# Seven block products for eight in the down projection of a gated feed-forward, and the feed-forward cut into an up phase and a down phase for each half of the tokens

## The chip, the core and the metric

The kernel runs on one core of one Trainium2 chip. The metric is the device time of one execution in microseconds (us); the median of the runs counts. TensorE (PE in the profile) does the matrix products, ScalarE (ACT) the activation functions and plain copies, VectorE (DVE) and GpSimd (POOL) the elementwise work, and SyncE (SP) issues nearly all DMAs, one after the other, from one queue. PE writes its sums into PSUM, which has 8 banks of 128 x 512 fp32 numbers; everything else lies in SBUF or in DRAM.

## The reference, cut to what matters

```python
xn = _layernorm(x)                    # x: 2048 tokens x 640
s  = _A_ref(xn, wqkv, w_phi, wo)      # 32 heads of linear attention: softmax features of q and k, then @ wo
h  = gelu(xn @ w1 + b1)               # 640 -> 1536
g  = silu(h @ w2 + b2)                # 1536 -> 640
return x + s * g
```

All of it is fp32. The kernel computes each large product to nearly that precision with three passes of the faster fp32r format: an operand a is kept as `hi` (a rounded to fp32r) and `lo = a - hi`, and the product is hi*hi + hi*lo + lo*hi. So every operand of a large product needs a copy (`hi`, on ACT) and a subtraction (`lo`, on DVE or POOL) before PE can use it, and PE runs three matmuls for one product of 128 x 128 weights with 512 columns.

## The kernel before, in words

Time runs in three stages.

The **first stage** normalizes and transposes x and computes k, v and q and the features of k and q. It ends with the exponentials of q in DRAM (`e_dram`) and with x in two forms in SBUF: `xp` (the eight blocks of x, as hi and lo) and `xd` (nine sums and differences of those blocks). One half of the tokens (1024) lies there at a time; both halves are also in DRAM (`xp_dram`, `xd_dram`).

The **feed-forward stage** is a loop over 12 units: 2 halves of the tokens times 6 groups `g` of 256 of the 1536 hidden features. The order of all instructions on all engines is the order in which the program writes them; nothing is reordered. A unit has two parts.

- Up: the 256 x 640 by 640 x 1024 product for the group, as seven block products for eight (Strassen's scheme in Winograd's form) over two column blocks of 512 tokens and two of 128 features. `PARTS` lists the seven; `part` (L1191 to L1202) issues 6 matmuls for a block product, 9 where the odd fifth block of 128 of the 640 is added: 54 in a unit. ACT and DVE put the results together (`keep` L1217, sums at L1488 to L1508), `act` (L1205) applies the Gelu in the PSUM bank and copies the `hi` part to SBUF, and `act_lo` (L1212) subtracts, with PSUM as one source.
- Down: `down` (L1222 to L1240) multiplies the group's 256 hidden features with w2, for 512 tokens and then for the other 512, into five blocks of 128 outputs: 2 x 5 x 2 x 3 = 60 matmuls. Each of the ten results of a unit is only a partial sum over 256 of 1536 features, so DVE adds it to a running sum `y` in SBUF (L1239; a plain copy, L1237, in the first group).

Beside that run, spread over the unit with generators that `next` advances: the w2 weights of a unit are loaded whole and split by ACT and POOL (L136, L138); the w1 weights of the next unit are loaded and their sums and differences formed and split (L589 to L601; in the second half most come back from DRAM instead, `w1_back`); the queries of 16 token tiles are normalized (`q_norm`, L1285: two products over 128 x 1280 on POOL, two sums over heads and some small work on DVE) and stored as `phi_dram`; at the end of the first half `reload` brings the second half of x from DRAM; after it the gates of the first half go through the Silu to `g_dram` (L1472).

The **last stage** goes over four chunks of 512 tokens. `num_t` (L1324, L1327) transposes the query features, `num_m` (L1335 to L1339) multiplies them with the state of the keys, `finish` (L1402 to L1405) multiplies with wo (15 matmuls for one of five output blocks), by the gate, and adds x. The first chunk's transposes and state products lie inside the last unit's down part (`last_mid`), as do the splits of wo.

SBUF is given out from pools of equal buffers: `slabs` (23 of 5 KB per partition), `rows` (11 of 2.75 KB), and `xp`, `xd`. A tile that finds no free buffer waits until an older tile's last reader is done, and what is queued behind it on its engine, or on SP, waits too.

## Time and profile before

| | |
|---|---|
| time, median of 3 runs (lowest, highest) | 661.1 us (660.86, 661.21) |
| profiled execution, from the first to the last instruction | 659.8 us |
| PE busy, PE weight loads busy | 652.2 us, 572.6 us |
| DVE, POOL, ACT busy | 449.2, 392.8, 325.4 us |
| DMA, mean over the span | 198 GB/s |
| feed-forward stage, from the chain of waits | 238.42 to about 559.7 us |

The profiled execution's own time is given only as its span; the runs' median stands 1.3 us above that span. A row of the groups of instructions reads: line, engine, operation, output tile <- input tiles, shape, count | busy time, mean duration of one | idle time of that engine just before them and who ended it. Matmuls overlap, so the mean duration of one (about 390 ns) is not the time that one adds; the chain of waits, which merges successive work of one line into a piece with a start, a length and a count, gives that.

### The profile page before, as it was taken

Reading aid. Unit: us, or ns where it says so; the run is one execution under the profiler, and the core shown is the slowest. Engines: PE = TensorE matmul, PEld = TensorE weight load, DVE = VectorE, ACT = ScalarE, POOL = GpSimd, SP = SyncE. Lnnn points to the kernel's source line nnn. Section 1 sums busy time; section 2 is a strip of 40 time slices with the busy share of each in tenths; the row PEclk is TensorE's granted clock in tenths of the full one; section 3 lists DMA queues with packets and bytes.
Section 4 is the critical chain, followed back from the end, with each engine's and each line's share of the span. In section 5 each row is a group of like instructions: output and inputs, shape, how many; then the busy total and the mean of one; then the engine's idle time right before and its main releaser. Section 6 shows DMA issues by size and latency. Waiting matters only on the chain.

```text
span 659.8 us, 11974 instructions
## 1 busy us (share of the span) xinstructions
PE 652.2 (99%) x4616; PEld 572.6 (87%) x4616; DVE 449.2 (68%) x714; ACT 325.4 (49%) x550; POOL 392.8 (60%) x344
## 2 busy tenths in 40 slices
PE   8999999999999999999999999999999999999997
PEld 8999999999999998888888888888888887877876
DVE  5878987766885756595885685777967877333132
ACT  4556777644666678435245138632132336645320
POOL 3597887774883437776875754746357665422322
PEclk9999999999999999999999999999999999999999
DMA  8436912031924882539656697456375275668444
GB/s 319 184 121 205 294 63 67 27 102 37 299 87 147 312 310 81 198 118 321 222 178 246 249 425 290 167 223 243 120 283 199 81 307 230 209 215 316 139 133 148
DMA packets 77081, 130.62 MB, mean 198 GB/s; under 512 B 5056, under 2 KB 44480, under 8 KB 76128
## 3 DMA queue, kind: packets, MB, share of 16 engines
q1 hardware_dynamic: 76704, 129.20, 55.0%
q10 hardware_dynamic: 320, 0.66, 0.6%
q8 instruction: 36, 0.59, 0.3%
q14 instruction: 21, 0.17, 0.1%
HBM read 81.66 MB, written 46.20 MB: 194 GB/s over the span
## 4 chain that ended last, share of the span: by engine, by line
PE 94%; POOL 2%; DMA 1%; issue 1%; DVE 1%; ACT 0%; SPq 0%; POOLq 0%
PE pB L1230 25%; PE pB L1201 22%; PE pW L485 20%; PE pB L1402 10%; PE pA L344 4%; PE pW L977 3%; PE pB L1335 3%; PE pB L1324 2%; PE pA L163 2%; PE kv L577 1%; DMA folds<-in_wqk_dram 1%; POOL tt L276 1%; POOL xd L295 0%; PE pB L1342 0%; PE pA L330 0%
## 5 line engine op out<-in xcount | busy, mean ns | idle before, releaser
L1230 PE MATMUL pB<-hs,w2s 128*128 128x512 f32 x720 | 167.0, 390 | 0.0
L1230 PEld LDWEIGHTS pB<-hs,w2s 128*128 128x128 f32 x720 | 134.6, 188 | 28.2 <-DVE oT L1339 0.4
L1201 PE MATMUL pB<-xp,w1s 128*128 128x512 f32 x324 | 81.3, 389 | 0.0
L1201 PE MATMUL pB<-xd,w1s 128*128 128x512 f32 x324 | 79.3, 389 | 0.0
L1239 DVE TENSOR_TENSOR y<-pB,y 128x512 f32<-128x512 f32 x100 | 63.7, 680 | 15.8 <-PE pB L1230 15.6
L1402 PE MATMUL pB<-oT,wo 128*128 128x512 f32 (+1 forms) x315 | 72.5, 385 | 0.2
L1201 PEld LDWEIGHTS pB<-xd,w1s 128*128 128x128 f32 x324 | 60.8, 188 | 12.6
L1201 PEld LDWEIGHTS pB<-xp,w1s 128*128 128x128 f32 x324 | 60.8, 188 | 12.6
L1206 ACT ACTIVATE pB<-pB,b1t 128x512 f32<-128x512 f32 x48 | 31.8, 662 | 77.6 <-DVE pB L1497 28.3
L1402 PEld LDWEIGHTS pB<-oT,wo 128*128 128x128 f32 x315 | 56.1, 188 | 13.0 <-DVE oT L1339 1.2
L402 POOL TENSOR_TENSOR eq<-eq,rc 128x1280 f32<-128x1280 f32 x16 | 37.9, 2369 | 48.7 <-DVE rc L1301 43.8
L383 POOL TENSOR_TENSOR e<-e,mxs 128x1280 f32<-128x1280 f32 x13 | 30.7, 2372 | 41.4 <-DVE mxs L378 25.7
L389 ACT ACTIVATE e<-e 128x1280 f32<-128x1280 f32 x32 | 40.8, 1274 | 17.9 <-POOL e L383 8.3
L601 POOL TENSOR_TENSOR w1s<-raw,w1s 128x640 fp32r<-128x640 f32 (+1 forms) x18 | 24.9, 1386 | 41.2 <-ACT w1s L600 41.1
L485 PE MATMUL pW<-wsum,xd 128*128 128x320 f32 x288 | 48.4, 310 | 0.0
L1288 POOL TENSOR_TENSOR ez<-eq,zrep 128x1280 f32<-128x1280 f32 x16 | 47.3, 2954 | 0.0
L1217 ACT ACTIVATE x<-pB 128x512 f32<-128x512 f32 x12 | 7.2, 600 | 78.9 <-PE pB L1201 78.9
L485 PEld LDWEIGHTS pW<-wsum,xd 128*128 128x128 f32 x288 | 43.6, 188 | 0.0
L138 POOL TENSOR_TENSOR w2s<-raw,w2s 128x640 fp32r<-128x640 f32 x24 | 37.1, 1567 | 7.1 <-ACT w2s L136 7.1
L402 POOL TENSOR_TENSOR e<-e,rc 128x1280 f32<-128x1280 f32 x15 | 36.1, 2410 | 5.8 <-DVE rc L838 4.2
L1327 ACT ACTIVATE ph<-pB 120x512 f32<-120x512 f32 (+1 forms) x44 | 22.9, 604 | 26.5 <-PE pB L1324 23.8
L1212 DVE TENSOR_TENSOR hs<-pB,hs 128x512 fp32r<-128x512 f32 x48 | 32.0, 685 | 5.2 <-ACT hs L1208 5.0
(216 smaller groups left out, 1282.1 us busy)
## 6 DMA issues: line engine op xcount, KB each, us to landing
raw<-in_w_dram SPq DMA_DIRECT2D x42, 320.0 KB
e_dram<-e SPq DMA_DIRECT2D x16, 640.0 KB
eq<-e_dram SPq DMA_DIRECT2D x16, 640.0 KB
phi_dram<-eq SPq DMA_DIRECT2D x16, 640.0 KB
phi<-phi_dram SPq DMA_DIRECT2D x16, 640.0 KB
xt<-in_x_dram SPq DMA_DIRECT2D x16, 320.0 KB
xres<-in_xt_dram SPq DMA_DIRECT2D x20, 256.0 KB
out_dram<-xres SPq DMA_DIRECT2D x18, 256.0 KB
```

Source lines behind the costliest of these rows:

```text
L138: eng.tensor_tensor(sl[:, 1, :], raw, sl[:, 0, :].bitcast(F32), op=OP.subtract)
L383: eng.tensor_tensor(e3, e3, mx[:, :, None].to_broadcast([P, 64, DH]), op=OP.subtract)
L389: nc.scalar.activation(ef, ef, AF.Exp)
L402: eng.tensor_tensor(e3, e3, rc[:, :, None].to_broadcast([P, 64, DH]), op=OP.mult)
L485: nc.tensor.matmul(self.bank[ch][:, :HALF], self.x(blk, a), w(b), start=new and i == 0, stop=i == len(mms) - 1, skip_group_check=True)
L1201: nc.tensor.matmul(bank[ch][:], tl[:, a, off + wo_:off + wo_ + P], mov(blk, b), start=new and n == 0, stop=n == len(mms) - 1, skip_group_c ...
L1206: nc.scalar.activation(ps, ps, AF.Gelu_apprx_tanh, bias=b1t[:, f:f + 1])
L1212: nc.vector.tensor_tensor(hs[:, 1], ps, hs[:, 0].bitcast(F32), op=OP.subtract)
L1230: nc.tensor.matmul(ps[:], ws[i][:, b, d * P:(d + 1) * P], hs[o][i][:, a, :], start=i == n == 0, stop=(i, n) == (GF - 1, 2), skip_group_che ...
L1239: nc.vector.tensor_tensor(y, ps[:], y, op=OP.add)
L1288: nc.gpsimd.tensor_tensor(zv, ef, zf, op=OP.mult)
L1402: nc.tensor.matmul(ps[:, cols], w, o[:, a, cols], start=n == 0, stop=n == 14)
```

## The change

The down product leaves the loop over groups. For each half of the tokens, `up` runs for all six groups and keeps the Gelu's results in SBUF, unsplit (`raws`); then `down` runs once, over all 1536 features, also in seven block products: the features are cut into the first and the second 128 of each group, four of the five output blocks into two pairs, the 1024 tokens into two blocks of 512. Each block product is 6 groups x 2 output blocks x 3 passes = 36 matmuls, accumulated over all groups in the same two PSUM banks. The fifth output block is done in the plain way, mixed in (72 matmuls in a half, as before). A half then has 7 x 36 + 72 = 324 down matmuls, where it had 360.

What this adds: differences of the kept activations (`T1` to `T4`, on POOL, 24 in a half); for each of 42 operands in a half (7 kinds x 6 groups) a `form`: a copy into a PSUM bank and a `hi` copy on ACT, then `lo` on DVE with the bank as source (the first six of a half go without the bank); sums and differences of w2, formed once, split and stored to DRAM (`s_dram`), from where they are loaded in each half; and the plain parts of w2, loaded and split in each half, with `lo` on DVE. The running sums `y` in SBUF are gone: the ten gates of a half are made in one go from PSUM (`gate_out`) and stored, so all the gates come back from DRAM in the last stage.

The side work is no longer advanced by generators but hung on numbered slots: `when(s, f, ...)` files a call, `tick` runs those of a slot in the order in which they were filed. There are 7 slots in an `up`, one after each block product, and 42 in a `down`, one after each operand. The w1 sums of the first half are now needed every 54 matmuls. In the second half of the feed-forward two of the four w1 tiles of a group are loaded and split again and two come from DRAM. The reload of x is spread over the first `down`, and for 256 of its tokens the nine sums are made again from `xp` on POOL instead of going to DRAM (`plan_x`). Eight of the query tiles are normalized beside the second `up` phase, two beside the first `down`, four beside the second, two in the last stage. The first chunk's transposes stand in slots 27 to 37 of the second `down`, its state products in slot 38, the splits of wo in slots 26 to 38.

The pools change: `slabs` has 10 buffers, 13 more (`lead`) serve only the first stage, and a string `HOMES` says for each allocation of that stage which of the two it takes. `lead` and `rows` are then closed and their room goes to 21 `cells` of 4 KB (activations, operands, w1 tiles) and 6 `halves` of 2 KB.

The diff, cut to its core:

```diff
-    slabs = ctx.enter_context(tc.tile_pool(name="slabs", bufs=23))
-    rows = ctx.enter_context(tc.tile_pool(name="rows", bufs=11))
+    slabs = ctx.enter_context(tc.tile_pool(name="slabs", bufs=10))
+    early = ExitStack()
+    lead = early.enter_context(tc.tile_pool(name="lead", bufs=13))
+    rows = early.enter_context(tc.tile_pool(name="rows", bufs=11))
...
+        pool = slabs if next(homes, "S") == "S" else lead
...
-            nc.scalar.activation(sl[:, 0, :n], src, AF.Copy)
-            nc.gpsimd.tensor_tensor(sl[:, 1, :n], src, sl[:, 0, :n].bitcast(F32), op=OP.subtract)
+            (split or split_now)(src, sl[:, 0, :n], sl[:, 1, :n], nc.gpsimd if lo[len(out)] == "pool" else nc.vector)
...
-    PARTS = (("X", "A11", 0, None), ("Y", "S2", 10, None), ("X", "A12", 2, ("A1k", 4)), ("V", "S3", 12, ("A2k", 7)),
-             ("Z", "S1", 8, None), ("W", "A22", 14, ("A2k", 16)), ("Z", "S4", 5, ("A1k", 7)))
+    PARTS = (("X", "A11", 0, None), ("Y", "S2", 10, None), ("V", "S3", 12, ("A2k", 7)), ("Z", "S1", 8, None),
+             ("X", "A12", 2, ("A1k", 4)), ("W", "A22", 14, ("A2k", 16)), ("Z", "S4", 5, ("A1k", 7)))
...
+    def split_late(src, hi, lo, eng):
+        nc.scalar.activation(hi, src, AF.Copy)
+        after(1, lambda: eng.tensor_tensor(lo, src, hi.bitcast(F32), op=OP.subtract))
...
+    UP0, DN0, UP1, DN1, OUT = 0, 42, 84, 126, 168
...
+    def form(n, lo):
+        k, g = FORMS[n]
+        while k in SUM and (k, g) not in sums_done:
+            sum_step()
+        src = block(k, g)
+        hs = cell((P, 2, CW), F32R, "hs")
+        if lo == "bank":
+            ps = bankB()
+            nc.scalar.activation(ps[:], src, AF.Copy)
+        nc.scalar.activation(hs[:, 0], src, AF.Copy)
+        ring[k, g] = hs
+        def low():
+            (nc.gpsimd if lo == "pool" else nc.vector).tensor_tensor(
+                hs[:, 1], ps[:] if lo == "bank" else src, hs[:, 0].bitcast(F32), op=OP.subtract)
+            sums_due.extend([(t, g) for t in dict(B11=("T2",), B21=("T4",), T2=("T1",)).get(k, ())])
+        after(1, low)
...
+    def plan_w(s):
+        for i, k in enumerate(("A11", "A12", "S2", "S3", "S1", "S4", "A22")):
+            for d in range(3):
+                use = s + 6 * i + 2 * d
+                if i == 0:
+                    when(use - 8, w_load, "A5", d)
+                    when(use - 5, w_make, "A5", d)
+                if k in SUMS:
+                    when(use - 6, w_sum, k, d)
+                else:
+                    when(use - 7, w_load, k, d)
+                    when(use - 4, w_make, k, d)
...
+        def step():
+            n = at_step[0]
+            at_step[0] += 1
+            form(n + AHEAD, los(n + AHEAD))        # AHEAD = 6
+            sum_step()
+            tick()
...
+        def run(banks, k, f, start, e=None, lead=0):
+            for g in range(NG):
+                if e is not None:
+                    bank, c, es, et = e
+                    for i in range(lead + 1) if g == 0 else (g + lead,):
+                        if i < NG:
+                            mm3(bank, col("A5", i, c), ring[f, i], es and i == 0, et and i == NG - 1)
+                h = ring.pop((f, g))
+                for i in range(2):
+                    mm3(banks[i], col(k, g, i), h, start and g == 0, g == NG - 1)
+                if g < NG - 1:
+                    step()
...
+    def plan_q(t, s, pace=(-4, 0, 1, 3, 4, 7)):
+        for f, k in zip((q_load, q_ez, q_rc, q_dn, q_scale, q_store), pace):
+            when(s + k, f, t)
...
+    for g in range(1, NG):
+        s = UP0 + 7 * (g - 1)
+        if g > 1:
+            when(s - 4, w1_next, g)
+        when(s + 1, w1_sums, g)
+        for i, k in enumerate((2, 3, 4, 6)):
+            when(s + k, w1_step, g)
+        for i in range(2):
+            when(s + 7 + i, w1_put, g, i)
+    for g in range(NG):
+        plan_s(g, (7, 13, 20, 27, 34, DN0 + 2)[g])
...
+    plan_q(0, DN0 + 5)
+    plan_q(1, DN0 + 9)
...
+    for i in range(4):
+        when(DN0 + 2 + 4 * i, reload, i)
+        when(DN0 + 18 + 4 * i, reload, 4 + i)
```

More of the change, by code (lines that the diff above doesn't have):

```diff
@@ new lines, in add, with when, after, tick @@
+    def add(out, a, b, eng=nc.vector, op=OP.add):
+        eng.tensor_tensor(out, a, b, op=op)
+    todo, at_slot = {}, [0]
+    def when(s, f, *args):
+        assert s >= at_slot[0]
+        todo.setdefault(s, []).append((f, args))
+    def after(k, f, *args):
+        when(at_slot[0] + k, f, *args)
+    def tick():
+        for f, args in todo.pop(at_slot[0], ()):
+            f(*args)
+        at_slot[0] += 1
+    def load(dst, src):
+        nc.sync.dma_start(dst, src)
+    def store(k, dst, src):
+        after(k, load, dst, src)
@@ L1577, in hedgehog_gated_mlp_kernel, with w1_next, w1_step @@
-    hs = (None, (h12, h22))
-    load_res(0)
-    load_res(1)
-    for _ in down(g, w2g, hs, 1, groups):
-        pass
-    for _ in q2:
-        pass
-    gate(0)
-    gate(1)
-    late_store[0] = True
-    for ci, c in enumerate(ORDER):
+            store(1, out_t[d * P:(d + 1) * P, c * CW:(c + 1) * CW], xr[:])
+    def w1_next(g):
+        w1r_at[g] = load_w1(g, lambda *a: slab(a[1], a[2], a[0]))
+    def w1_step(g):
+        out = next(w1f_at[g])
+        if out is not None:
+            w1g_at[g], w1_tiles[g] = out, out["tiles"]
@@ new lines, in hedgehog_gated_mlp_kernel @@
+    for g in range(NG):
+        s = UP1 + 7 * (g - 1)
+        when(s - 3, w1_raw, g)
+        when(s - 1, w1_sum_tiles, g)
+        when(s + 1, w1_wa, g)
+        when(s + 3, w1_wb, g)
+    when(UP1 + 9, kv_state, kvr_out[0])
+    for i in range(8):
+        plan_q(2 + i, UP1 - 1 + 5 * i)
+    down(2, LO)
+    for g in range(NG):
+        up(g)
+    xstack.close()
+    tailp.append(ctx.enter_context(tc.tile_pool(name="late", bufs=8, side="right", reuse_waits="tile")))
+    tailp.append(ctx.enter_context(tc.tile_pool(name="phs", bufs=14, side="right", reuse_waits="tile")))
```

643 lines of the change are left out of this document (342 added, 301 removed).

## The prediction

> **What bounds the kernel now.** First the page: who is busy, and at what clock.
>
> ```profile
> PE 652.2 (99%) x4616; PEld 572.6 (87%) x4616; DVE 449.2 (68%) x714; ACT 325.4 (49%) x550; POOL 392.8 (60%) x344
> PEclk9999999999999999999999999999999999999999
> ```
>
> PE is busy for all but 7.6 us. A busy PE can still be a waiting one, so next the chain of waits in order of time (start, length, piece):
>
> ```profile
> 64.32 2.19 issue
> ...
> 266.47 12.24 PE pB L1201 x54
> 278.71 13.60 PE pB L1230 x60
> ...
> 548.67 0.61 PE pB L1324 x8
> ...
> 556.98 1.62 PE pB L1230 x6
> ...
> 559.02 1.96 DMA oT<-oTl
> 560.99 0.74 ACT wo L136
> ...
> 561.79 1.58 POOL wo L138
> ...
> 563.41 0.73 PE pB L1402 x2
> ...
> 565.35 3.52 PE pB L1402 x15
> ```
>
> In the feed-forward PE alternates between 54 up matmuls and 60 down matmuls without a gap: 12.24 / 54 and 13.60 / 60 both give 0.2267 us for one. That is the price of a matmul of 512 columns in this kernel, whichever operands it has. The busy time by stage says the same:
>
> ```profile
> 252.80:395.70 142.90, 142.90 (x632) 118.20 (x631) 105.35 (x148) 59.14 (x96) 104.67 (x82) 1.00 0.65 235
> 421.90:537.50 115.60, 115.60 (x512) 95.72 (x511) 88.98 (x141) 35.96 (x56) 71.80 (x39) 1.00 0.52 193
> ```
>
> (Columns: stretch, length, PE, PE's weight loads, DVE, ACT, POOL, clock, DMA share, GB/s.) PE 142.90 of 142.90. So a matmul taken out of this stage is worth its whole 0.2267 us, as long as its side work keeps up; DVE and POOL stand at 74% and 73% there, ACT at 41%.
>
> The chain ends the stage with a detour through a DMA, ACT and POOL from 558.60 to 563.41, 4.8 us. It isn't 4.8 us of idle PE, as PE's timeline shows:
>
> ```profile
> 556.91 3.06 PE L1230 MATMUL pB<-hs,w2s 128*128 128x512 f32 x12
> 559.81 4.34 PE L1402 MATMUL pB<-oT,wo 128*128 128x512 f32 x15
> ```
>
> Most of the 15 ran during the detour. Undisturbed, 15 take 3.52 (the chain at 565.35); these end at 559.81 + 4.34 = 564.15 where 556.98 + 12 x 0.2267 + 3.52 = 563.22 was possible. The wait for oT and the last wo costs 0.9 us.
>
> **The change part by part.** *Matmuls.* The down product falls from 12 x 60 = 720 to 2 x (7 x 36 + 72) = 648; up, transposes, state and wo products keep their number. 72 x 0.2267 = **-16.3 us**, all on the path that sets the end.
>
> *End of the feed-forward.* State products and the last wo split move to slot 38 of the second down, with three operands (18 matmuls, 4.1 us) still to run. The 1.96 of the DMA and 0.74 + 1.58 of the split, side by side, fit. **-0.9** (bounds -0.9 to 0).
>
> *Side work* costs nothing where it fits under PE and stalls where it doesn't. Its prices:
>
> ```profile
> L1208 ACT ACTIVATE hs<-pB 128x512 fp32r<-128x512 f32 x48 | 28.8, 600 | 2.1
> L600 ACT ACTIVATE w1s<-st 128x512 fp32r<-128x512 f32 x18 | 10.6, 622 | 0.5 <-POOL st L589 0.5
> L1391 ACT ACTIVATE y<-y,b2t 128x512 f32<-128x512 f32 x10 | 7.0, 724 | 3.0 <-DMA oT<-oTl 3.0
> L1327 ACT ACTIVATE ph<-pB 120x512 f32<-120x512 f32 x40 | 20.9, 606 | 14.0 <-PE pB L1324 11.3 <-issue 2.7
> L136 ACT ACTIVATE w2s<-raw 128x640 fp32r<-128x640 f32 x24 | 16.8, 735 | 11.6 <-DVE dn L397 9.2 <-PE pB L1230 1.7 <-DMA xd_dram<-xhi 0.7
> L1212 DVE TENSOR_TENSOR hs<-pB,hs 128x512 fp32r<-128x512 f32 x48 | 32.0, 685 | 5.2 <-ACT hs L1208 5.0 <-issue 0.2
> L601 POOL TENSOR_TENSOR w1s<-st,w1s 128x512 fp32r<-128x512 f32 x18 | 23.0, 1296 | 0.0
> L589 POOL TENSOR_TENSOR st<-raw 128x256 f32<-128x256 f32 x18 | 13.3, 741 | 7.4 <-DMA w_dram<-w1s 5.0 <-DMA raw<-in_w_dram 2.4
> L1288 POOL TENSOR_TENSOR ez<-eq,zrep 128x1280 f32<-128x1280 f32 x16 | 47.3, 2954 | 0.0
> L402 POOL TENSOR_TENSOR eq<-eq,rc 128x1280 f32<-128x1280 f32 x16 | 37.9, 2369 | 48.7 <-DVE rc L1301 43.8 <-issue 4.9
> ```
>
> *First up phase.* A unit is now 12.24 us, no longer 25.84, and must hold the w1 forms of the next one. POOL: four w1 sums (3.0), two lows (2.6), the w2 sums (four of 256 columns and one of 128, about 3.3), one difference (1.3): 10.2 of 12.24. DVE: five sums of 0.685 (3.4) and lows over 640 + 384 + 2 x 512 + 128 = 2176 columns. These lows have both sources in SBUF, and here two engines get in each other's way:
>
> ```profile
> 168.27 0.83 DVE L138 TENSOR_TENSOR wq<-rq,wq 128x640 fp32r<-128x640 f32 x1
> 169.52 3.82 DVE L138 TENSOR_TENSOR wq<-rq,wq 128x640 fp32r<-128x640 f32 x2 [0.43 <-ACT wq L136]
> 168.94 3.72 POOL L138 TENSOR_TENSOR wq<-rq,wq 128x640 fp32r<-128x640 f32 x2 [2.03 <-ACT wq L136]
> ```
>
> Alone, DVE's subtraction takes 0.83 for 640 columns (1.3 ns each); with POOL at the same work two take 3.82. Undisturbed, 2176 columns are 2.8 us. If they only pass through POOL's gaps, the pair needs 10.2 + 2.8 = 13.0 in 12.24, 0.8 too much, in five units 4.0. The w1 tiles come two to four slots ahead (2.7 to 8 us), which absorbs part. Bounds **0 to 4.0**; I take 1.2, nearer nothing, since a first unit without w2 sums lets POOL get ahead. (The Trainium skill, page "SBUF — State Buffer", section "Who interferes with whom", says that a VectorE tensor_tensor with both inputs in SBUF and a GpSimd operation that reads SBUF exclude each other for a whole instruction. The 3.82 agrees. By the rule the sum would carry the 4.0 in place of 1.2.)
>
> *First down phase* (324 x 0.2267 = 73.4 us of PE, 1.36 or 2.04 a slot). ACT: 36 forms of 0.600 + 0.622 = 44.0, twelve weight copies 7.5, ten gates 7.2, some 3 besides: 62 of 73.4. No row has an ACT copy from SBUF to PSUM; between 0.600 and 0.724, I take 0.600 as the nearest (a plain copy). DVE: 36 x 0.685, twelve lows of 0.67 and a dozen sums are 41, which leaves 32 for the head sums of two query tiles. POOL is the tight one: in the first 18 slots (32.6 us) 18 differences of 1.3 (23.4), a 19th, the last w2 sums (3.3), two query tiles (2 x (2.954 + 2.369) = 10.6): 38.6, so 6 us late at slot 18. The T1 differences filed at slots 12 to 17 are operands at 24 to 29, 20 us later; SP's `q_store` in slot 16 waits for POOL and holds weight loads needed 12.2 us later. DMA moves in these slots, from the shapes, 4.2 MB of x, 3.1 of w2 sums, 2.6 of queries and some 2.8 others: 12.7 MB, 390 GB/s. What it can carry is the reload of before, from 375 to 400 us:
>
> ```profile
> DMA packets 1626, 10.55 MB, mean 422 GB/s; under 512 B 177, under 2 KB 177, under 8 KB 729
> ```
>
> So it is hidden, narrowly: the lead of 12.2 us covers it and POOL's 6, and without that lead each us late would cost one. **0 to 2**, I take 0.3.
>
> *Second up phase*: POOL has one query tile in 9.6 us (5.3) and little else; nothing. *Second down phase*: as the first, plus on ACT the first chunk's copies. In slots 24 to 35 ACT has 12 forms (14.7), two gates (1.4), nine `ph` (5.5), four wo copies (2.9), two weight copies (1.2): 25.7. PE has 20.4 and nine transposes of 0.31 (half of the 0.61 for eight above): 23.2. ACT falls 2.5 behind (3.7 with 0.724 for the copy to PSUM). Operands are made six slots ahead, but a transpose takes a PSUM bank that a late form must give back, so PE can wait here. **0 to 3.7**, I take 1.2.
>
> *First stage.* 23 slabs become 10 and 13 by a fixed list, which can only add waits for a free buffer; two loads to the first unit's w2 go. The nearest price is a transfer of 640 KB, 1.6 us at 422 GB/s. **-1.4 to 3.1** (two such transfers; below nothing, should waits like the 2.19 at 64.32 fall otherwise), I take 0.
>
> *Last stage.* Ten more gate loads (2.6 MB over 91 us), two query tiles, ten Silus fewer on ACT:
>
> ```profile
> 564.20:655.60 91.40, 91.40 (x564) 73.23 (x561) 28.94 (x79) 34.27 (x78) 28.07 (x37) 1.00 0.62 206
> ```
>
> DMA 206 + 29 GB/s, POOL 28 + 11 of 91: nothing.
>
> **Sum**: 659.8 - 16.3 - 0.9 + 1.2 + 0.3 + 1.2 + 0 = 645.3 us for the profiled execution; the median stands 1.3 above the span, so **646.6 us**. The bounds are 643.9 - 1.4 = 642.5 and 643.9 + 4.0 + 2 + 3.7 + 3.1 = 656.7.
>
> **The rivals.** *Nothing stalls*: 661.1 - 17.2 = **643.9**. For it: PE ran gapless with DMA at 422 GB/s and POOL at 73%. Against it: every unit has half the time for w1.
>
> *The first up phase paces itself*: POOL and DVE exclude each other, 13.0 a unit, and the two downs come in at two thirds of their bounds: 643.9 + 4.0 + 3.8 = **651.7**. For it the 3.82 above; against it, that w1 tiles come slots ahead and the first unit gains some 4 us.
>
> *Slower: POOL's queue holds SP.* In the downs everything on POOL is late, `q_store` waits at the head of SP's queue, the reload of `xd` waits for that store, and the weights of S1 and S4 stand behind both. A weight load filed at slot 18 (32.6 us into the phase) is needed 12.2 later and takes some 2, so SP must be free by 42.6. `q_scale`, filed at slot 13 (25.8), takes 2.4: PE stands once POOL is 14 us late there, and then one us for one. I forecast 6. POOL at 1.2 times its rows is 38.6 x 1.2 - 32.6 = 13.7 late, just the point; at 1.43 times 22.6, which costs 8.6 in each down and eats the 17.2. At 1.5 times it is 25.3, 2 x 11.3 = 22.6, **666.5**. For it:
>
> ```profile
> L138 POOL TENSOR_TENSOR w2s<-raw,w2s 128x640 fp32r<-128x640 f32 x24 | 37.1, 1567 | 7.1 <-ACT w2s L136 7.1
> L138 POOL TENSOR_TENSOR wq<-rq,wq 128x640 fp32r<-128x640 f32 x2 | 3.7, 1880 | 2.0 <-ACT wq L136 2.0
> ```
>
> the same operation stretched from 1567 to 1880 beside a DVE at the same work, 1.2 times. Against it: that is the most any row shows.
>
> *The change doesn't do what it says*: side matmuls or stalls spread evenly give the 17 us back, **661**. Counting in the code speaks against it.
>
> **How the numbers follow.** Forecast (645 to 650) 0.48; nothing stalls 0.20; first up phase 0.17; POOL's queue 0.12; no gain 0.03. A difference under 0.2% (1.3 us) can't be told from none. So faster 0.85, same 0.03, slower 0.12. The range takes in the bounds, 642.5 to 656.7, and reaches a little on, to 659; what lies above is most of the last two cases.
>
> **What would show it.** Down matmuls 648 in number and still 0.2267 apart; the down phases as unbroken pieces of 73.4 us, the up phases of 73.4 as well (6 x 12.24). First up phase right: PE's gaps there under 2 us in sum, ended by a w1 tile. Second down: PE waiting before the transposes for ACT, 1 us or so. Wrong: a down phase over 76 us, PE ended by a w2 weight or an operand; SP standing on a store for more than 10 us; matmuls further apart than 0.2267.

## The result, and the profile after

The changed kernel takes 671.4 us (median; 670.28 to 672.46) against 661.15 beside it on the same chip: 1.015 times as long, 95% interval 1.0134 to 1.0165. It is slower; 646.6 was forecast. The page of its profile (busy times; what DMA moved; the chain of waits by engine):

```profile
PE 646.4 (97%) x4544; PEld 559.1 (84%) x4544; DVE 467.2 (70%) x702; ACT 380.3 (57%) x681; POOL 440.2 (66%) x382
...
DMA packets 86411, 154.63 MB, mean 231 GB/s; under 512 B 6320, under 2 KB 47792, under 8 KB 85840
...
PE 70%; DVE 14%; POOL 7%; issue 5%; DMA 2%; ACT 2%; SPq 0%; POOLq 0%; DVEq 0%; ACTq 0%
```

PE has the 72 matmuls less that the change promised (4616 to 4544), yet its busy time fell by 5.8 us only, and 30% of the chain that ended last is no longer PE (6% before). DMA moves 154.63 MB in place of 130.62. Busy time by stage (stretch, length, PE, PEld, DVE, ACT, POOL, clock, DMA share, GB/s), first before: feed-forward, last stage.

```profile
238.20:559.80 321.60, 321.60 (x1469) 264.90 (x1468) 235.64 (x359) 140.24 (x221) 205.77 (x138) 1.00 0.60 222
559.80:655.60 95.80, 95.59 (x580) 75.94 (x578) 32.99 (x84) 37.46 (x81) 29.63 (x38) 1.00 0.60 197
```

After: first up, first down, second up, second down, last stage.

```profile
238.60:314.20 75.60, 75.60 (x326) 60.82 (x326) 52.11 (x66) 49.40 (x81) 66.98 (x64) 1.00 0.78 285
314.20:397.90 83.70, 78.50 (x333) 63.16 (x332) 58.68 (x77) 58.54 (x111) 62.58 (x49) 0.98 0.90 322
397.90:473.90 76.00, 76.00 (x329) 61.11 (x327) 65.14 (x97) 28.42 (x47) 59.10 (x29) 1.00 0.67 247
473.90:564.60 90.70, 84.30 (x414) 66.42 (x413) 72.23 (x102) 65.28 (x125) 56.83 (x33) 1.00 0.79 273
564.60:665.10 100.50, 97.39 (x580) 75.98 (x578) 38.45 (x94) 30.89 (x72) 37.66 (x41) 1.00 0.69 237
```

What PE would need without a stall: 324 x 0.2267 = 73.45 in every phase, in the first down 2.15 more for the eight matmuls of `kv_norm`, in the second up 0.3 for the state's transposes, in the second down 8 for transposes and state products (eleven groups of four transposes at 0.27; 0.56 and 4.32 in the chain). For the last stage, before's 95.8 less its 0.9 of waiting.

| us | first up | first down | second up | second down | last stage |
|---|---|---|---|---|---|
| without a stall | 73.45 | 75.6 | 73.7 | 81.4 | 94.9 |
| forecast | 74.65 | 75.9 | 73.7 | 82.6 | 94.9 |
| after | 75.6 | 83.7 | 76.0 | 90.7 | 100.6 |
| over the forecast | 1.0 | 7.8 | 2.3 | 8.1 | 5.7 |

Together 24.9, where 671.4 - 646.6 = 24.8. (Smaller ones cancel: the median stands 2.4 above the span and not 1.3; the feed-forward of before had itself lost 1.1 against its count of matmuls.) So the question is not where one big loss is, but what five phases lose, each in its way.

**The up phases** have no gap, and yet take longer. PE's timeline (start, length, then what ran) before:

```profile
276.51 2.20 PE L1201 MATMUL pB<-xp,w1s 128*128 128x512 f32 x9
278.55 1.75 PE L1230 MATMUL pB<-hs,w2s 128*128 128x512 f32 x7
```

and after:

```profile
270.09 2.26 PE L1198 MATMUL pB<-xp,w1s 128*128 128x512 f32 x9
272.19 2.26 PE L1198 MATMUL pB<-xd,w1s 128*128 128x512 f32 x9
274.29 3.66 PE L1198 MATMUL pB<-xp,w1s 128*128 128x512 f32 x15
```

From start to start nine matmuls took 2.04 (0.2267 each); now 2.10 (0.2333), at a granted clock of 1.00. The instructions are the same; what differs is where `xp` and `xd` lie. In before, 32 fp32 of padding stood ahead of `xp` (L56, `xpad`), and `xp` and `xd` began at multiples of 256 bytes in each partition. The change drops the padding with the new pools, and both begin 96 bytes beyond one; so do the `wo` weights of the last stage. (These starts follow from the order in which the program gives out SBUF; no profile shows them. The runs below show what shifting them does.)

**The first down** stands three times. The chain of waits there (start, length, piece):

```profile
318.58 10.25 PE pB L1390 x45
...
330.14 1.20 DVE ws L1243
331.34 3.36 DVE w2s L1243
334.70 1.41 DVE rc L404
...
345.79 2.97 POOL qroom L1524
...
348.79 1.50 DVE dn L404
...
351.38 1.17 DVE den L1536
...
353.71 0.69 DVE hs L1313
...
354.44 43.63 PE pB L1390 x184
```

An operand's low part (`hs`, 0.69) stands in DVE's queue behind a query tile's head sum (`dn`), which waits for POOL's product (`qroom`, 2.97). DVE is busy nearly throughout, in the second down too (the first and the last line; the one between is the rest of the first down):

```profile
334.70:355.10 20.40, 15.20 (x64) 11.26 (x63) 18.91 (x27) 13.84 (x25) 16.35 (x11) 1.00 0.76 243
355.10:398.00 42.90, 42.90 (x184) 35.32 (x183) 23.62 (x36) 27.85 (x51) 26.85 (x25) 0.96 0.92 332
...
495.00:515.00 20.00, 16.29 (x71) 12.78 (x70) 19.69 (x25) 11.61 (x21) 19.52 (x13) 1.00 0.72 212
```

DVE 18.91 of 20.40 and 19.69 of 20.00.

PE's waits in the first down come to 5.2 us of the 8.1 lost. Another 1.9 is no wait: the last 184 matmuls fill 43.63 us where 184 x 0.2267 are 41.7. The granted clock is below 1.00 there, as the line between shows (0.96). In steps of 2 us it is 0.50 from 356 to 358, soon after the wait of 2.9 us, 0.69 in the next step, and 1.00 from 360 on. So the low clock comes on top of the wait. The remaining 1.0 us was not placed.

The operation that was costed at 0.67 us, the low part of w2, is among them (group, busy time, mean ns):

```profile
L1243 DVE TENSOR_TENSOR w2s<-w2r,w2s 128x512 fp32r<-128x512 f32 x24 | 27.5, 1150 | 0.6 <-ACT w2s L1242 0.6
```

**The last stage**: PE waits for the transfer of oT, in brackets the wait.

```profile
587.23 3.78 PE L1635 MATMUL pB<-oT,wo 128*128 128x512 f32 x15
592.26 1.94 PE L1635 MATMUL pB<-oT,wo 128*128 128x512 f32 x6 [1.26 <-DMA oT<-oTl]
594.64 2.35 PE L1635 MATMUL pB<-oT,wo 128*128 128x512 f32 x9 [0.44 <-DMA oT<-oTl]
```

The 15 matmuls from 587.23 are done at 591.01; the next wait until 592.26, then until 594.64. One output block, 3.5 us, is all the cover that the transfer has. A third wait for oT, at 621, makes 3.1 us of waiting in all.

### The profile page after: what moved, and what is told of

It reads as the page before. It is cut to its first block, busy times and chain, and to the rows that moved or that the text cites. A ratio compares the mean times of both kernels' runs of the same rounds, so it can differ in the third digit from the quotient of the medians.

```text
span 669.0 us, 12217 instructions
## 1 busy us (share of the span) xinstructions
PE 646.4 (97%) x4544; PEld 559.1 (84%) x4544; DVE 467.2 (70%) x702; ACT 380.3 (57%) x681; POOL 440.2 (66%) x382
## 2 busy tenths in 40 slices
DMA packets 86411, 154.63 MB, mean 231 GB/s; under 512 B 6320, under 2 KB 47792, under 8 KB 85840
## 4 chain that ended last, share of the span: by engine, by line
PE 70%; DVE 14%; POOL 7%; issue 5%; DMA 2%; ACT 2%; SPq 0%; POOLq 0%; DVEq 0%; ACTq 0%
PE pW L492 20%; PE pB L1198 14%; PE pB L1390 13%; PE pB L1635 9%; PE pA L351 4%; POOL ez L1524 3%; DVE dn L404 3%; PE pW L975 3%; DVE w2s L1243 2%; PE pB L1562 2%; PE pA L170 2%; DVE hs L1313 1%; DMA oT<-oTl 1%; PE pB L1573 1%; PE kv L584 1%
## 5 line engine op out<-in xcount | busy, mean ns | idle before, releaser
L1390 PE MATMUL pB<-hs,w2s 128*128 128x512 f32 x648 | 155.1, 396 | 10.6 <-DVE w2s L1243 5.6
L1390 PEld LDWEIGHTS pB<-hs,w2s 128*128 128x128 f32 x648 | 121.0, 189 | 39.6 <-DVE w2s L1243 7.4
L1250 ACT ACTIVATE hr<-pB,b1t 128x512 f32<-128x512 f32 x48 | 32.8, 686 | 68.2 <-DVE pB L1219 67.6
L1638 POOL TENSOR_TENSOR xres<-gt,xres 128x256 f32<-128x256 f32 x36 | 25.7, 735 | 57.2 <-issue 30.6
L1313 DVE TENSOR_TENSOR hs<-pB,hs 128x512 fp32r<-128x512 f32 x72 | 46.6, 678 | 14.1 <-ACT hs L1309 14.0
L1637 DVE TENSOR_TENSOR gt<-pB,gt 128x256 f32<-128x256 f32 x40 | 15.3, 420 | 58.9 <-PE pB L1635 56.0
L1308 ACT ACTIVATE pB<-hr 128x512 f32<-128x512 f32 x72 | 42.2, 586 | 21.9 <-DVE hs L1313 16.6
L1309 ACT ACTIVATE hs<-hr 128x512 fp32r<-128x512 f32 x84 | 52.0, 620 | 4.4 <-PE pB L1390 4.4
L1295 POOL TENSOR_TENSOR hr<-hr 128x512 f32<-128x512 f32 x36 | 50.2, 1422 | 0.0
L1524 POOL TENSOR_TENSOR ez<-eq,zrep 128x1280 f32<-128x1280 f32 x14 | 42.1, 3006 | 1.5 <-PE pB L1390 1.5
```

The lines of the kernel that those rows point to most:

```text
L1250: nc.scalar.activation(dst, ps, AF.Gelu_apprx_tanh, bias=b1t[:, f:f + 1])
L1295: nc.gpsimd.tensor_tensor(block(k, g), block(a, g), block(b, g), op=OP.subtract)
L1308: nc.scalar.activation(ps[:], src, AF.Copy)
L1309: nc.scalar.activation(hs[:, 0], src, AF.Copy)
L1313: (nc.gpsimd if lo == "pool" else nc.vector).tensor_tensor(hs[:, 1], ps[:] if lo == "bank" else src, hs[:, 0].bitcast(F32), op=OP.subtract)
L1390: nc.tensor.matmul(ps[:], w(b), hs[:, a, :], start=start and n == 0, stop=stop and n == 2, skip_group_check=True)
```

## The experiments

Stage lengths are read from PE's timelines as above, the time is the median beside the runs of the kernel before on the same chip (661.2 to 662.2). "Aligned" is the kernel of after with its operands at multiples of 256 bytes again; it is the base of all rows below it.

| us | first up | first down | second up | second down | last | time | ratio, 95% interval |
|---|---|---|---|---|---|---|---|
| after | 75.6 | 83.7 | 76.0 | 90.7 | 100.6 | 671.4 | 1.015 (1.0134 to 1.0165) |
| aligned | 73.7 | 83.1 | 75.5 | 90.9 | 100.8 | 668.6 | 1.010 (1.0073 to 1.0126) |
| aligned, six query tiles not normalized in the downs | 73.7 | 81.7 | 75.5 | 85.2 | 99.0 | 658.8 | 0.9948 (0.9927 to 0.997) |
| the same, and no reload of xp | 73.9 | 75.6 | 75.5 | 85.2 | 98.8 | 655.3 | 0.9906 (0.9887 to 0.9926) |
| aligned, w2's low parts from a bank | 74.9 | 82.9 | 76.4 | 87.5 | 98.1 | 666.0 | 1.0061 (1.0044 to 1.0077) |
| aligned, two blocks of cover | 74.6 | 83.1 | 75.5 | 90.9 | 96.0 | 664.7 | 1.0039 (1.0021 to 1.0056) |
| all three edits, queries 0/9/4/3, lows on POOL | 73.7 | 75.6 | 80.3 | 95.0 | 101.8 | 671.6 | 1.0144 (1.0129 to 1.016) |
| reload later, queries 2/8/4/2 | 74.0 | 81.7 | 77.4 | 85.9 | 95.8 | 659.7 | 0.9962 (0.9947 to 0.9977) |
| queries 0/9/5/2 | 73.6 | 75.7 | 76.3 | 91.4 | 94.9 | 657.1 | 0.9931 (0.9914 to 0.9947) |
| queries 0/9/4/3 | 73.8 | 75.6 | 76.3 | 87.1 | 97.4 | 655.4 | 0.9918 (0.9898 to 0.9938) |
| queries 0/10/4/2 | 74.0 | 78.4 | 75.5 | 89.6 | 95.5 | 658.1 | 0.9948 (0.9931 to 0.9965) |

(Queries a/b/c/d: tiles planned for the first down, second up, second down, last stage.) Stages with the same code differ between these profiles. The first up phases of the aligned kernels lie between 73.6 and 74.9. The last stage with one block of cover and two query tiles goes from 98.1 to 100.8 in five kernels, with two blocks from 94.9 to 96.0 in four. So about a microsecond in an up phase, or less than 3 us in a last stage with one block of cover, is not argued from.

### Where the operands start

The kernel of after with 96 bytes of padding ahead of `xpool`, which puts `xp`, `xd` and `wo` at multiples of 256:

```diff
+    ctx.enter_context(tc.tile_pool(name="pad", bufs=1, side="right")).tile([P, 24], F32, name="rpad")
     xpool = xstack.enter_context(tc.tile_pool(name="xpool", bufs=1, side="right", reuse_waits="tile"))
```

> The changed kernel with 96 bytes of unused SBUF put on the right side ahead of the pool that holds xp and xd, so that xp, xd and later the split wo start at a multiple of 256 bytes as in the kernel before; in the changed kernel they start 96 bytes beyond one. Address theory: the matmuls that stream xp and xd take 0.2333 us there against 0.2267 before because of that start, so each up phase falls from 75.6 to 73.4 us and the finishing products of the last stage from 0.2387 to 0.2347: 2 x 2.2 + 300 x 0.004 = 5.6 us, time 671.4 - 5.6 = 665.8. Rival, load: the matmuls are slowed by the busier DMAs and engines beside them: up phases stay at 75.6 and the time at 671. Both expect the stalls of the down phases to stay.

The kernel of before with more padding, `xp` 96 and `xd` 64 bytes beyond a multiple of 256:

```diff
-    xpool.tile([P, 32], F32, name="xpad")
+    xpool.tile([P, 56], F32, name="xpad")
     xp = xpool.tile([P, 8, 2, CW], F32R, name="xp")
+    xpool.tile([P, 56], F32, name="dpad")
```

> The kernel before with the unused 128 bytes ahead of xp made 224 and 224 more between xp and xd, so that xp starts 96 and xd 64 bytes beyond a multiple of 256; nothing else moves. Address theory: up matmuls at 0.2333 us, a unit's 54 at 12.60 in place of 12.24, 12 units: +4.3 us, 665.4; if only one of the two starts matters, only the matmuls of that tile slow down and the time is 663.3. Rival, load: no change, 661.1.

And once more before, with 64 and 40 in place of 56 and 56 (`xp` 128 bytes beyond, `xd` 32):

> The kernel before with the activations at other starts: xp 128 bytes beyond a multiple of 256 (96 in the run of the first call), xd 32 (64 there). The run with 96 and 64 gave 2.10 us for nine up matmuls on xp (0.2333 each) and 1.39 for six, 3.44 for fifteen on xd (0.2317 and 0.2293), against 0.2267 in the kernel before. If any start off a multiple of 256 costs the same, xp and xd both stay at 0.2317 to 0.2333 and the time is 665 to 667. If the distance from a multiple of 64 or 128 decides, xp at 128 goes back to 0.2267 and xd at 32 stands at 0.229 to 0.233; the time is then 662.5 to 664. All other stages as before.

Aligned, the first up phase of after falls from 75.6 to 73.7 and the time by 2.9 us, where 5.6 was expected; the second falls only from 76.0 to 75.5, since something else holds it there, and the last stage not at all. Before with 96 and 64 takes 666.1 us (ratio 1.0068, 1.005 to 1.0085), a unit 12.53 and not 12.24. With 128 and 32, 665.9 us (1.0065, 1.0048 to 1.0082), a unit 12.57:

```profile
296.00 2.26 PE L1202 MATMUL pB<-xp,w1s 128*128 128x512 f32 x9
298.10 1.56 PE L1202 MATMUL pB<-xd,w1s 128*128 128x512 f32 x6
299.49 0.86 PE L1202 MATMUL pB<-xp,w1s 128*128 128x512 f32 x3
300.19 3.66 PE L1202 MATMUL pB<-xd,w1s 128*128 128x512 f32 x15
303.69 2.26 PE L1202 MATMUL pB<-xp,w1s 128*128 128x512 f32 x9
```

From start to start, nine on `xp` at 128 take 2.10, as at 96, and fifteen on `xd` at 32 take 3.50: 0.2333 both. (At 64 the fifteen took 3.44, 0.2293, and six took 1.39, 0.2317.) Padding and nothing else makes the kernel before 4.4 us slower: the start address is shown as the cause, 32, 96 and 128 cost some 6 to 7 ns a matmul, and "the distance from a multiple of 64 or 128 decides" is out, since 128 costs as much as 96. Why 64 costs less stays open.

### The downs: DVE, DMA or both

On the aligned kernel, the products and head sums of the six query tiles in the downs are left out (tiles 0, 1, 10 to 13 are loaded and stored unnormalized):

```diff
-            when(s + k, f, t)
+            if f in (q_load, q_store) or t not in (0, 1, 10, 11, 12, 13):
+                when(s + k, f, t)
```

> As the aligned kernel, but the six query tiles that are normalized beside the two down phases (0, 1 and 10 to 13) are loaded and stored without the normalization: its products on POOL and sums and small operations on DVE are left out, loads and stores stay. DVE theory: in the down phases the operands' and weights' subtractions stand in DVE's queue behind head sums (5.4 us a tile on DVE) and behind sums that wait for POOL; without them the first down falls from 83.6 to about 76 and the second from 90.8 to about 82: 15 us, so 651. Rival, weights late: SP's queue or the DMAs bring the weights late; the downs keep most of their stalls and the time falls by less than 4 us, to 662 or more.

The second down falls by 5.7 (the theory had 9), and the time by 9.8, below before. But the first down falls by 1.4 only, and what ends its one stall is new:

```profile
316.93 42.08 PE pB L1391 x185
359.01 7.57 DMA w2s<-s_dram
...
366.72 3.36 PE pB L1391 x8
```

A weight's transfer, which PE waits for: 4.0 us of wait. The eight matmuls behind it take 0.42 each, at a granted clock of 0.50 from 368 to 370; that loses another 1.9 by the end of the phase (114 matmuls in 27.73 for 25.8). DMA's share is around 1 for most of the first 60 us of that phase. So, with the same edit, the four reloads of `xp` were left out as well (the second half then works on the first half's blocks):

```diff
-        when(DN0 + 2 + 4 * i, reload, i)
```

> The kernel without the normalization of six query tiles in the downs, and now also without the four reloads of the first eight blocks of x in the first down (4.2 MB); the second half then works on the first half's blocks. The first down took 81.7 us there, 6.1 above its work of 75.6, with PE's one long wait on a w2 sum's transfer of 7.6 us. Theory (the DMA engines are full there, share 0.97 to 1.03, and weights come behind 4.2 MB of x): the first down falls to 75.6 to 77, the other stages stay within 0.7 us. Rival (ACT's high parts or the order of the forms make the wait): it stays above 80.

The first down takes 75.6, its bare work. In the stretch where PE had stood, first with the reloads and then without:

```profile
360.00:375.00 15.00, 10.97 (x41) 8.61 (x41) 5.98 (x11) 6.40 (x12) 10.60 (x12) 0.89 1.03 353
```

```profile
360.00:375.00 15.00, 15.00 (x68) 12.43 (x67) 9.18 (x15) 11.26 (x21) 12.46 (x14) 1.00 1.07 381
```

At this place DMA is as full without them; it is from 330 to 345 that its share is lower (0.78 for 1.02), and the weights then come in time. Next the same from the other side. With the two tiles normalized again, the reload begun later, half of the first down's w2 lows (and all of the second's) from a bank, two blocks of cover for oT (both below) and later head sums in the second half, the question was whether DMA alone held the first down:

```diff
-        when(DN0 + 2 + 4 * i, reload, i)
-        when(DN0 + 18 + 4 * i, reload, 4 + i)
+        when(DN0 + 10 + 3 * i, reload, i)
+        when(DN0 + 22 + 3 * i, reload, 4 + i)
...
-        plan_x(p, DN0 + 22 + 7 * p)
+        plan_x(p, DN0 + 24 + 7 * p)
```

> The aligned kernel of after with two blocks of cover for oT and the query tiles left where the change puts them (two in the first down, eight in the second up phase, four in the second down, two at the end), but with a longer way between ez and the head sums that read it (4 slots for 3), the reload of x in the first down begun at slot 10 and issued every third slot (from slot 2 and every fourth before), and the low parts of w2 for A12 and A22, and all of the second down's, subtracted from a PSUM copy. Theory (the first down stands on DMA, the second on DVE's two-SBUF lows and on its queue): first down 78 to 81 (83.1), second 86 to 88 (90.9), last stage 96, the time 656 to 661. Rival (in the first down it is DVE's queue that sets the end): first down over 82, the time 661 to 665.

81.7, between what the two foresaw (up to 81, over 82). No transfer is named in its chain; DVE and POOL are:

```profile
342.49 2.97 POOL qroom L1533
...
345.48 1.50 DVE dn L405
...
350.39 0.69 DVE hs L1314
...
351.13 42.38 PE pB L1399 x178
```

PE's one wait is 3.6 us, for that `hs`, and the 178 matmuls behind it again take 2.0 more than their count. So two limits of nearly the same size lie on each other in the first down: take away the query tiles' work on POOL and DVE, and the transfers cost 6 us; spread the transfers, and DVE's queue costs 6. It is clean where both give way: above, without the query tiles' work and the reload, and below, without the query tiles, work and transfers both, the reload kept.

### w2's low parts from a bank

Subtracting from SBUF costs DVE 1150 ns. Here ACT copies the raw w2 to a PSUM bank first, and DVE reads that:

```diff
-        split_late(wraw.pop((k, d))[:], t[:, :, 0, :], t[:, :, 1, :], nc.gpsimd if lo == "pool" else nc.vector)
+        src, ps = wraw.pop((k, d))[:], bankB()
+        p3 = ps[:].rearrange("p (g c) -> p g c", g=2)
+        nc.scalar.activation(p3, src, AF.Copy)
+        nc.scalar.activation(t[:, :, 0, :], src, AF.Copy)
+        after(1, lambda: nc.vector.tensor_tensor(t[:, :, 1, :], p3, t[:, :, 0, :].bitcast(F32), op=OP.subtract))
```

> As the aligned kernel, but the 24 splits of plain w2 weights copy the raw weights to a PSUM bank on ACT first and subtract on DVE from that bank, as the activations' operands do. Theory of the shared port: DVE's subtraction with both sources in SBUF takes 1.15 us in the mean (up to 3.4, when POOL is in the middle of an operation) against 0.69 from a bank, and what it holds up in DVE's queue is what PE waits for; 24 x 0.46 = 11 us less on DVE, of which about half is stall: 660. Rival, DVE simply has too much: the gain is below 2 us, since the head sums stay. Third: the bank that it takes is missed by PE, and the time rises.

```profile
L1334 DVE TENSOR_TENSOR w2s<-pB,w2s 128x512 fp32r<-128x512 f32 x24 | 16.4, 685 | 4.4 <-ACT w2s L1333 4.3
```

685 for 1150: 11.1 us less of DVE over both downs. The second down gains 3.4, and PE's wait for `w2s` there is 0.7 us (4.2 in after). The first down gains 0.2 only. The up phases measured 1.1 and 0.9 longer, hardly more than the same code varies. It is 2.6 us in all by the medians, to 666.0 where 660 was expected, and the two intervals of the ratio overlap a little (1.0073 to 1.0077).

### The cover of oT

```diff
-            nxt = num_groups(phin, oTn, ((4, 0), (4, 0), (3, 0), (0, 11)))
+            nxt = num_groups(phin, oTn, ((5, 0), (6, 0), (0, 11)))
```

> The aligned kernel of after, with one edit in the last stage: the eleven transposes of the next chunk are made in two steps (5, 6) and not three (4, 4, 3), so the state products, and the transfer of oT behind them, are issued one output block earlier and have two blocks of 15 matmuls (7.0 us) to land in, not one (3.5). Theory (the stalls at 577 and 605 us are that transfer, 4.8 us in landing with 3.5 of cover): the last stage falls from 100.8 to 96.5 to 98, the time by 3 to 4.5 us, to 664 to 666. Rival (the transfer is slow because the DMA engines are full, and whatever is asked first comes late): the stage stays within 1 us of 100.8 and PE waits for another transfer, an xres or a gate.

The last stage falls by 4.8 to 96.0 against the aligned kernel's 100.8 (by 2.1 against the shortest stage with one block), the time by 3.8. PE's waits for oT are 0.9 us; in the aligned kernel they were 2.3, with 0.9 more for a gate's product and some 1.7 by a granted clock of 0.50 from 594 to 596. No other transfer took their place.

```profile
581.48 8.49 PE L1636 MATMUL pB<-oT,wo 128*128 128x512 f32 x36
590.82 2.32 PE L1636 MATMUL pB<-oT,wo 128*128 128x512 f32 x9 [0.85 <-DMA oT<-oTl]
```

36 matmuls stand where 15 stood.

### All of it, and where the query tiles can go

All three edits, and the queries moved (the room of `xd`, which the first down's two tiles had used, is given back earlier): nine tiles in the second up phase from five slots before it, four in the second down, three in the last stage; the low parts of w2 of the second down's first operands (A5, A11) on POOL.

```diff
-    plan_q(0, DN0 + 5)
-    plan_q(1, DN0 + 9)
...
-    for i in range(8):
-        plan_q(2 + i, UP1 - 1 + 5 * i)
+    for i in range(9):
+        plan_q(i, UP1 - 5 + 5 * i, (-3, 0, 1, 3, 4, 7))
```

> The aligned kernel of after with the causes found so far taken out together, all work kept: no query tile in the first down (nine in the second up phase, four in the second down, three in the last stage), low parts of w2 in the downs subtracted from a PSUM copy made on ACT (those made in the last up unit of the second half on GpSimd), and two blocks of cover for oT. Theory (the 31 us between what 648 matmuls save and the time measured are DVE in both downs, DMA in the first, and oT's cover at the end): first down 76 to 80, second 83 to 86, last stage 96 to 99, up phases 73.5 to 75.5; the time 650 to 657, below the kernel before. Rival (the side work only stalls PE in another place, the second up phase or the end): the second up phase over 78 or the last stage over 101, and the time 660 to 667.

The rival came out, and worse than it had it: 671.6, where its range was 660 to 667. The first down is clean, but second up and second down take 80.3 and 95.0, the latter at a mean granted clock of 0.96. PE's longest wait in the second down is the first weight's low part, late in POOL's queue: 4.4 us for w2s. In the up phase the chain holds two eq transfers of 7.8 and 10.1 us and then goes again and again from POOL's `ez` (2.96) to the head sum that waits for it in DVE's queue (1.50) and on to a sum of the up product, as in the first down of after. The next kernels put the A5 and A11 lows on DVE from a bank, load eq a slot earlier, and give the head sums four slots after `ez`, not three (`pace` below). These were not tried apart. With five tiles in the second down and two in the last stage:

```diff
+    for i in range(9):
+        plan_q(i, UP1 - 5 + 5 * i, (-4, 0, 2, 4, 5, 8))
...
+    for i in range(5):
+        plan_q(9 + i, DN1 + 4 + 5 * i, (-3, 0, 2, 4, 5, 7))
```

> As the kernel beside it, but with no query tile in the first down: nine in the second up phase from five slots before it, five in the second down, two in the last stage; the reload of x stays at slot 2 and every fourth, in the order of after. Theory (without the queries' 2.6 MB the first down is clean, 75.6; the longer way between ez and its head sums keeps DVE from standing behind GpSimd): first down 75.6 to 77, second up phase 75.5 to 78, second down 86 to 89, last stage 96; the time 652 to 658. Rival (the ninth tile in the second up phase and the fifth in the second down cost as much as the two cost in the first down): the second up phase over 79 or the second down over 91, the time 660 or more.

657.1 us. The first down is as the matmuls are counted:

```profile
312.80 2.04 PE pB L1399 x9
314.84 2.15 PE pB L1173 x8
316.99 71.50 PE pB L1399 x315
```

324 in 73.54, 0.2270 each. The second down, with the fifth tile, takes 91.4. Then four there and three in the last stage,

```diff
-        plan_q(9 + i, DN1 + 4 + 5 * i, (-3, 0, 2, 4, 5, 7))
+        plan_q(9 + i, DN1 + 4 + 5 * i, (-3, 0, 2, 4, 5, 8))
...
+        plan_q(13 + i, OUT + 1 + 2 * i, (-1, 0, 0, 1, 2, 3))
```

> As the kernel without a query tile in the first down, but with four tiles in the second down and three in the last stage (five and two before). Theory (the second down lost 10 us there because DVE was busy 38 of 40 us from 480 to 520, and took 85.9 with four tiles): second down 85 to 87, last stage 95 to 98, the time 651 to 655. Rival (the last stage, where DMA stood at a share of 0.9 and more to 600, gives the gain back): last stage over 100, the time 657 or more.

or ten in the second up phase, two of them begun in the first down, four and two:

```diff
+    for i in range(10):
+        plan_q(i, UP1 - 9 + 5 * i, (-4 if i else -2, 0, 2, 4, 5, 8))
```

> The same with ten tiles in the second up phase, the first two of them begun in the last slots of the first down (where DVE was busy 60%), four in the second down and two in the last stage. Theory: first down 76 to 78, second up 76 to 77.5, second down 85 to 87, last stage 95, the time 652 to 655. Rival (eq's 1.3 MB for each tile beside the reload brings back the wait for a weight's transfer): first down over 79, the time 656 or more.

655.4 and 658.1. The last stage takes the third tile for 2.5 us, the second down had asked 4.3 for its fifth. But with four tiles at the same pace the second down takes 87.1 in one of the two kernels and 89.6 in the other, so the price of a tile is not known to better than 2.5 us. In the third kernel the two early tiles cost the first down 2.8, with PE waiting 2.1 for DVE's w2s, not for a transfer. The fastest that computes everything is by its median the 0/9/4/3 one, 0.8% below before; its interval overlaps that of 0/9/5/2. The stages:

```profile
239.10:312.90 73.80, 73.80 (x327) 60.73 (x326) 52.20 (x63) 49.19 (x80) 67.88 (x64) 1.00 0.80 289
312.90:388.50 75.60, 75.60 (x333) 62.33 (x332) 46.56 (x67) 61.27 (x117) 54.23 (x45) 1.00 0.94 334
388.50:464.80 76.30, 74.44 (x329) 60.96 (x328) 66.19 (x99) 30.35 (x51) 60.47 (x29) 1.00 0.70 259
464.80:551.90 87.10, 84.39 (x413) 66.48 (x412) 67.11 (x105) 70.04 (x133) 55.70 (x33) 1.00 0.81 280
551.90:649.30 97.40, 95.69 (x580) 75.87 (x578) 42.73 (x101) 30.22 (x72) 42.89 (x43) 1.00 0.76 258
```

## Why the prediction was wrong, step by step

**Matmuls, -16.3: right in number, wrong as a price for all.** 648 down matmuls, and 0.2270 each where nothing stalls. But "the price of a matmul of 512 columns in this kernel, whichever operands it has" is false: on `xp` and `xd` it became 0.2333 with the starts of those tiles, 2.1 in the first up phase, part of the 2.3 in the second, and some 1.3 in the 315 `wo` matmuls, 0.4 of it in the last 105 (20.87 to 21.30). My own row of before had spoken against it: 15 on `wo` in 3.52 are 0.2347 each. I read the pools' change for its buffers and waits only, and passed over the line of padding that the diff takes out.

**End of the feed-forward, -0.9: right.** The chain runs the last 18 down matmuls at 560.42 for 4.32 and the first 15 on `wo` from 564.74, without a gap.

**First up phase, 1.2: not needed.** With the starts mended it takes 73.7 for a bare 73.45, though POOL is busy 67 of 75.6. The w1 tiles' lead of two to four slots absorbed all of it, and the rival *the first up phase paces itself* falls.

**First down phase, 0.3: this step failed; it was 8.1.** Three sizes in it were wrong. DVE's twelve lows of w2 were taken at "0.67", the price with POOL idle, while the same text had POOL busy for the whole phase; they took 1.15. (Mended alone, this gave the first down 0.2 and the second 3.4, so it set the time in the second only.) (The Trainium skill, page "SBUF — State Buffer", section "Who interferes with whom", has a VectorE instruction with two SBUF inputs contend with a GpSimd instruction that reads SBUF, and one with at most one SBUF input not. The runs agree: 1150 ns from SBUF, 685 from a bank. I weighed the rule in the first up phase, where it cost nothing that shows, and not in the downs.) "41, which leaves 32" averaged DVE over 73 us; the query tiles, the w2 sums' splits and the operands' lows meet in 20 of them, where DVE is 93% busy, in a queue in which a head sum that waits for POOL holds an operand. And the 390 GB/s that were to be "hidden, narrowly" under 422 measured capacity by the reload of before alone; in the first down's full stretches DMA stands at a share of 0.92 to 1.03 while moving 303 to 386 GB/s. (The Trainium skill's page "DMA: Bandwidth & Descriptors", section "Specifications", gives 435 GB/s as the ceiling of the fabric. The 422 of before comes near it; the first down's transfers did not reach it in these stretches, at a full share.) The two causes hide each other: taking one away showed 1.4 us, taking both 7.5. And the step had no term for the clock, which after a long wait of PE took 1.9 us more.

**Second down, 1.2: this step failed too; it was 9.3.** I looked at ACT and the transposes in slots 24 to 35; there the chain has pieces of six matmuls every 1.74 us (1.46 and four transposes) and next to no loss. The loss is earlier, in 473.9 to 532, where PE is idle 6.2 us, and DVE's. Without four tiles' normalization 5.7 of it goes, with w2's lows from a bank 3.4.

**Second up, "nothing": 2.3**, the start address and POOL's and DVE's queues, which were not separated: aligned it still takes 75.5, as it does with nothing normalized in the downs, and what ends PE's short waits in the later kernels is a w1 low on POOL.

**Last stage, "nothing": 5.7.** Averages again: 206 + 29 GB/s over 91 us says nothing of 576 to 588, where DMA's share is near 1 and the 1.96 us of an oT transfer, a row that I had quoted, becomes 4.4 to 4.8. Its cover of 3.5 was never compared with it. PE's waits for it make 3.1 of the 5.7, the start of `wo` some 1.3; the rest was not placed. Two blocks of cover gave 4.8 back against the aligned kernel's profile, 3.8 in the median time.

**First stage, 0: right**, to 0.3.

**The rivals.** *Slower: POOL's queue holds SP* came nearest in time (666.5), but for another reason than the one found. SP did stand behind POOL (us in total, times, longest):

```profile
SPq L1236 <- POOL eq L409: 70.7, 13, 10.8
```

10.8 at the longest, in the second down. That is the sign which I had named for it (SP standing on a store for more than 10 us), and the other signs of being wrong came too: downs over 76 us, PE waiting for an operand, matmuls further apart. But PE's waits in this kernel name DVE, not a weight's transfer. What I had right there is that a late POOL matters through the queue behind it; the queue was DVE's. *Nothing stalls* and *no gain* fall with the result.

What stays open: the 5.7 us that the second down, and the 2.6 that the second up of the fastest kernel still lose; and after which waits of PE the granted clock falls. That it adds to the stall is shown by the matmuls of the first downs, 1.9 to 2.0 us longer than their count with no wait among them.

## What to carry to other kernels

When a change takes matmuls out of a kernel whose PE has no gaps, the side work must be laid against the remaining time in windows of 10 to 20 us and in the order of each engine's queue, not against a phase's total: ask for each operand what stands ahead of it, and what that waits for. Two resources near their limit in one stretch hide each other, so an experiment that takes one away and gains little has not cleared it. A stall is dearer than the wait that the profile names, when the granted clock falls after it. And when tiles move in SBUF, compare where the operands of the matmuls begin before anything else; a line of padding can be worth half a per cent.

## What was not expected of the hardware

The price of an fp32r matmul of 512 columns depends on where its moving operand starts in the partition: 226.7 ns at a multiple of 256 bytes, 232 to 233 at 32, 96 or 128 beyond, 229 to 232 at 64. On 648 up matmuls that is 4.4 us, 0.67% of this kernel, at an unchanged clock of 1.00, and no wait or gap shows it; only the spacing of the matmuls does. The weights' start seems to matter as well: with `wo` 96 beyond, 15 products take 3.58 us, with `wo` aligned 3.52, and `oT`, the moving operand, lies in another pool that the padding leaves alone. This rests on one shift.

A small VectorE operation can take several times as long beside GpSimd. `den`, 32 columns, from DVE's timeline in the first down of after:

```profile
342.48 0.19 DVE L1536 SCALAR_TENSOR_TENSOR den<-dn 128x32 f32<-128x32 f32 x1
```

0.19 us, and POOL has been idle since 339.6; nine us later, in the chain above at 351.38, the same step takes 1.17, beside four differences (`hr`) that POOL runs in 5.00 us, 1.25 each. By the rows of the head sums' small steps a query tile asks DVE for 1.0 us of them at 342 and for at least 2.6 at 350.

A wait of PE can cost more than its length. After waits of 2.9 us (first down of after), 4.0 (without the query tiles' work) and 3.6 (reload later), the granted clock in the slowest step of 2 us was 0.50, 0.50 and 0.55 and it was 1.00 again within 6 us of the wait's end, and the matmuls behind the wait took 1.9 to 2.0 us more than their count at 0.2267. After waits of 1.45 and 1.36 in after it stayed at 1.00; after two of 1.3 and 1.0 close together in the aligned kernel's last stage it fell to 0.50. Where the border lies was not tested.
